# First-block transposes of x and g moved to TensorE, second-block transposing loads spread over ticks, and dwq computed for two heads at once, in an attention forward and backward kernel

## Chip, cores and metric

One core of a Trainium2 chip. The metric is the device time of one execution in microseconds (us). A ratio is the mean time of one kernel's fast runs over the mean of the other's fast runs of the same rounds, so it is not quite the ratio of the medians that stand beside it. Times are compared only within a set.

## The reference

Two independent attention blocks A and B with a key and value cache; output and all gradients are wanted. B=8 batches, 96 query rows, D=640, H=32 heads, 512 cached keys, head size 128, bfloat16. For one block:

```python
q = (x @ wq).reshape(B, Sq, H, Dh).transpose(0, 2, 1, 3)
p = softmax(einsum("bhqd,bhkd->bhqk", q, k_cache) * Dh ** -0.5)
o = einsum("bhqk,bhkd->bhqd", p, v_cache)
out = o.transpose(0, 2, 1, 3).reshape(B, Sq, H * Dh) @ wo
# gradients: d x, d k_cache, d v_cache, d wq, d wo; the outputs of A and B are concatenated
```

## The kernel before

The program is a software pipeline. A *tick* is one (head, batch) pair: 256 ticks for block A, 256 for B. Every piece of work is put at a tick and a slot, sorted, and issued in that order on each engine. Heads come in pairs (16 ticks) and in groups of four (32 ticks), so the pattern of work repeats every 32 ticks. `HK` says in which tick, counted from the start of a pair, the work of a head stands: pA loads its weights, pB transposes them, pC projects q and dO, pD makes natural tiles, qA transposes O (0) and dQ (1) back, qB computes dwo, qD computes dwq.

```python
HK = [
    dict(pA=-10, pB=-7, pC0=[-6, -4], pC1=[-5, -3], pD1=-2, pD0=0, qA0=21, qA1=25, qB=[28, 25], qD=[(26, 0, 2), (27, 2, 5)]),
    dict(pA=-7, pB=-2, pC0=[-1, 3], pC1=[1, 2], pD1=3, pD0=6, qA0=29, qA1=33, qB=[36, 33], qD=[(34, 0, 2), (35, 2, 5)]),
]
# ... cut ...
    def setup_T(which_, c):          # xT or gT: 128 columns of x or grad_out, transposed on the way in
        def f():
            # ... cut: the tile, one buffer ...
            sp(nc.sync.dma_start_transpose(S[key][:, c, :], src_flat[:, c * 128:(c + 1) * 128]))
        return f
# ... cut ...
    for c in range(DC):              # DC = 5
        em.add(tick0 + (-10 if first else -11 + c // 3), SL_LOAD + 0.5, setup_T(0, c))
        em.add(tick0 + (-9 if first else -10 + (c + 1) // 3), SL_LOAD + 0.6, setup_T(1, c))
    em.add(tick0 + (8 if first else 22), SL_LOAD + 0.5, setup_nat(1))   # g_nat, 960 KB
    em.add(tick0 + (9 if first else 21), SL_LOAD + 0.5, setup_nat(0))   # x_nat, 960 KB
# ... cut ...
            for ci in range(ncn):    # qD: dwq of one head, 128 columns wide
                c = c_lo + ci
                for t in range(TT):  # TT = 6
                    nc.tensor.matmul(w_ps[:, ci * 128:(ci + 1) * 128], S["x_nat"][:, t, c * 128:(c + 1) * 128], dQnat[:, t * 128:(t + 1) * 128],
                                     start=(t == 0), stop=(t == TT - 1))
# ... cut ...
            j = h % HP               # c_s7: dK of two heads is evicted into one tile and stored
            if j == 0:
                st["dK_p"] = wk.tile([128, HP, KC * 128], BF16, name="dK_sb", bufs=3)
```

All loads and stores are issued from one in-order queue (`sp`).

Names used below: S_ps holds the scores q k^T of one tick, negm their negated row maximum, E_sb the exponentials, P_sb the probabilities, PT_sb their transpose, dS_sb the gradient of the scores. KT_p and VT_p are keys and values transposed on the way in, K_sb and V_sb the same as they lie in memory. x_nat and g_nat are x and grad_out as they lie in memory ("natural" tiles), xT and gT their transposes. dV_sb and dK_sb are gradients that wait to be stored. To evict is to copy a result of TensorE from its accumulator to working memory.

Of the kernel before, what the change touches and what calls it, by code (L numbers as in the profile page):

```python
# [10 lines left out]
F32 = mybir.dt.float32  # L11
BF16 = mybir.dt.bfloat16
# [3 lines left out]
class Emitter:  # L16
# [14 lines left out]
SL_LOAD = 0  # L31
# [8 lines left out]
SL_HEAD = 90  # L40
SL_GRP = 95
SL_SETUP = 96

OFF = dict(kt=-1, vt=2, vn=1, kn=4, dv=7, dk=10, s2=3, s3=3, s4=4, s5=5, s6=6, s7=7, s8=8)
HP = 2
HK = [
    dict(pA=-10, pB=-7, pC0=[-6, -4], pC1=[-5, -3], pD1=-2, pD0=0, qA0=21, qA1=25, qB=[28, 25], qD=[(26, 0, 2), (27, 2, 5)]),
    dict(pA=-7, pB=-2, pC0=[-1, 3], pC1=[1, 2], pD1=3, pD0=6, qA0=29, qA1=33, qB=[36, 33], qD=[(34, 0, 2), (35, 2, 5)]),
]
EV = dict(pB0="act", pB1="dve", pC00="act", pC01="act", pC10="act", pC11="dve", pD0="dve", pD1="dve", qA0="dve", qA1="dve", qB0="act", qB1="act", qD="dve", gU="act")  # L50
GSPREAD0 = 9
# [20 lines left out]
def build_block(tc, em, tick0, blk, x, kc, vc, wq, wo, g_all, out_all, dx, dk, dv, dwq, dwo, ident, ones, pools, HG=4, first=True, groups=None):  # L72
    nc = tc.nc
    B, Sq, D = x.shape
# [4 lines left out]
    TT = T // 128  # L79
# [32 lines left out]
    def bank(shape, dt, name):  # L112
        return ps.tile(shape, dt, name=name, tag="bank")
# [8 lines left out]
    def setup_T(which_, c):  # L122
        def f():
            key = "xT" if which_ == 0 else "gT"
            if c == 0:
                S[key] = const.tile([128, DC, T], BF16, name=key, bufs=1)
            src_flat = x_flat if which_ == 0 else g_flat
            sp(nc.sync.dma_start_transpose(S[key][:, c, :], src_flat[:, c * 128:(c + 1) * 128]))
        return f

    def setup_nat(which_):
        def f():
            key = "x_nat" if which_ == 0 else "g_nat"
            src_flat = x_flat if which_ == 0 else g_flat
            t_ = const.tile([128, TT, D], BF16, name=key, bufs=1)
            sp(nc.sync.dma_start(t_[:], src_flat.rearrange("(t p) d -> p t d", p=128)))
            S[key] = t_
        return f
# [3 lines left out]
            S["out_acc"] = const.tile([128, TT, D], F32, name="out_acc", bufs=1)  # L142
            S["dx_acc"] = const.tile([128, TT, D], F32, name="dx_acc", bufs=1)

    for c in range(DC):
        em.add(tick0 + (-10 if first else -11 + c // 3), SL_LOAD + 0.5, setup_T(0, c))
        em.add(tick0 + (-9 if first else -10 + (c + 1) // 3), SL_LOAD + 0.6, setup_T(1, c))
    em.add(tick0 + (8 if first else 22), SL_LOAD + 0.5, setup_nat(1))
    em.add(tick0 + (9 if first else 21), SL_LOAD + 0.5, setup_nat(0))

    def evac(eng, dst, src, sc=None):
        if eng == "act":
            nc.scalar.activation(dst, src, ACT.Identity, scale=(1.0 if sc is None else sc))
        else:
            if sc is None:
                nc.vector.tensor_copy(dst, src)
            else:
                nc.vector.tensor_scalar(dst, src, float(sc), None, op0=ALU.mult)

    def pA(h):  # L160
        def f():
            g, hh = h // HG, h % HG
            if hh == 0:
                G[g] = dict(wo_r=grp.tile([128, HG, D], BF16, name="wo_r", bufs=2))
            wo_h = G[g]["wo_r"][:, hh]
            sp(nc.sync.dma_start(wo_h, wo[h * 128:(h + 1) * 128, :]))
            j = h % HP
            if j == 0:
                wq_p = hd.tile([128, DC, HP * 128], BF16, name="wq_p", bufs=2)
                with nc.allow_non_contiguous_dma(reason="per-pair wq slice"):  # L170
                    sp(nc.sync.dma_start(wq_p[:], wq_v[:, :, h * 128:(h + HP) * 128]))
            else:
                wq_p = HS[(blk, h - j)]["wq_p"]
            HS[(blk, h)] = dict(wo_h=wo_h, wq_p=wq_p, wq_h=wq_p[:, :, j * 128:(j + 1) * 128])
        return f
# [248 lines left out]
    def qA(h, which):  # L424
        def f():
            st = HS[(blk, h)]
            src = st["OT_h"] if which == 0 else st["dQT_h"]
            dst = hd.tile([128, TT * 128], BF16, name="Onat" if which == 0 else "dQnat", bufs=1)
            st["Onat" if which == 0 else "dQnat"] = dst
            for t0 in range(0, TT, 8):  # L430
                nt = min(8, TT - t0)
                n_ps = bank([128, 8 * 128], BF16, "nat_ps")
                for i in range(nt):
                    nc.tensor.transpose(n_ps[:, i * 128:(i + 1) * 128], src[:, (t0 + i) * 128:(t0 + i + 1) * 128], ident[:])  # L434
                evac(EV["qA%d" % which], dst[:, t0 * 128:(t0 + nt) * 128], n_ps[:, 0:nt * 128])
        return f

    def qB(h, di):
        def f():
            st = HS[(blk, h)]  # L440
            Onat = st["Onat"]
            if "dwo_sb" not in st:
                st["dwo_sb"] = hd.tile([128, D], BF16, name="dwo_sb")
            dwo_sb = st["dwo_sb"]
            (c0, w) = dsplits[di]
            w_ps = bank([128, w], F32, "dwo_ps")
            for t in range(TT):
                nc.tensor.matmul(w_ps[:], Onat[:, t * 128:(t + 1) * 128], S["g_nat"][:, t, c0:c0 + w], start=(t == 0), stop=(t == TT - 1))  # L448
            evac(EV["qB%d" % di], dwo_sb[:, c0:c0 + w], w_ps[:])
        return f  # L450

    def qB_st(h):
        def f():
            sp(nc.sync.dma_start(dwo[h * 128:(h + 1) * 128, :], HS[(blk, h)]["dwo_sb"][:]))
        return f

    def qD(h, c_lo, c_hi):
        def f():
            st = HS[(blk, h)]
            dQnat = st["dQnat"]  # L460
            j = h % HP
            pr = HS[(blk, h - j)]
            if "dwq_sb" not in pr:
                pr["dwq_sb"] = hd.tile([128, DC, HP * 128], BF16, name="dwq_sb", bufs=1)
            dwq_sb = pr["dwq_sb"]
            ncn = c_hi - c_lo
            w_ps = bank([128, 4 * 128], F32, "dwq_ps")
            for ci in range(ncn):
                c = c_lo + ci
                for t in range(TT):  # L470
                    nc.tensor.matmul(w_ps[:, ci * 128:(ci + 1) * 128], S["x_nat"][:, t, c * 128:(c + 1) * 128], dQnat[:, t * 128:(t + 1) * 128],  # L471
                                     start=(t == 0), stop=(t == TT - 1))
            evac(EV["qD"], dwq_sb[:, c_lo:c_hi, j * 128:(j + 1) * 128], w_ps[:, 0:ncn * 128].rearrange("p (a b) -> p a b", b=128))
        return f

    def qD_st(h):
        def f():
            with nc.allow_non_contiguous_dma(reason="per-pair dwq slice"):
                sp(nc.sync.dma_start(dwq_v[:, :, h * 128:(h + HP) * 128], HS[(blk, h)]["dwq_sb"][:]))
        return f  # L480
# [7 lines left out]
    def gU(g, which, t, di):  # L488
        def f():
            acc = S.get("out_acc" if which == 0 else "dx_acc")  # L490
            (c0, w) = dsplits[di]
            o_ps = bank([128, w], F32, "o_ps")
            for hh in range(groups[g]):
                h = GH0[g] + hh
                src = HS[(blk, h)]["OT_h"] if which == 0 else HS[(blk, h)]["dQT_h"]
                rhs = G[g]["wo_r"][:, hh, c0:c0 + w] if which == 0 else HS[(blk, h)]["wqT_h"][:, c0:c0 + w]
                nc.tensor.matmul(o_ps[:], src[:, t * 128:(t + 1) * 128], rhs, start=(hh == 0), stop=(hh == groups[g] - 1))  # L497
            if g == NG - 1:
                if di == 0:
                    G[(g, which, t)] = wk.tile([128, D], BF16, name="ob", bufs=4)  # L500
                dst = G[(g, which, t)][:, c0:c0 + w]
            else:
                dst = acc[:, t, c0:c0 + w]
            if g == 0:
                evac(EV["gU"], dst, o_ps[:])
            else:
                nc.vector.tensor_tensor(dst, o_ps[:], acc[:, t, c0:c0 + w], op=ALU.add)  # L507
        return f
# [10 lines left out]
    for g in range(NG):  # L519
        h0 = GH0[g]  # L520
        for hh in range(groups[g]):
# [1 line left out]
            j = h % HP  # L523
            c0t = tick0 + (h - j) * B
            hk = HK[j]
            em.add(c0t + hk["pA"], SL_LOAD, pA(h))
            em.add(c0t + hk["pB"], SL_HEAD, pB(h))
            em.add(c0t + OFF["s5"], SL_LOAD, h_alloc(h))
            for si in range(NTS):
# [27 lines left out]
            for di in range(len(dsplits)):  # L557
                em.add(c0t + hk["qB"][min(di, len(hk["qB"]) - 1)], SL_HEAD + 1, qB(h, di))
            em.add(c0t + max(hk["qB"]) + 2, SL_LOAD + 0.3, qB_st(h))
            if j == HP - 1:  # L560
                em.add(c0t + max(q[0] for q in hk["qD"]) + 2, SL_LOAD + 0.3, qD_st(h - j))
            em.add(c0t + hk["qA1"], SL_HEAD, qA(h, 1))
            for (k_, c_lo, c_hi) in hk["qD"]:
                if c_lo < DC:
                    em.add(c0t + k_, SL_HEAD + 2, qD(h, c_lo, min(c_hi, DC)))
        cLg = tick0 + (h0 + groups[g]) * B - 1
        gs0 = max(3, (GSPREAD0 * groups[g]) // HG)
        gs1 = max(3, (GSPREAD1 * groups[g]) // HG)
# [131 lines left out]
```

## Time and profile before

| | before |
|---|---|
| median at first, three runs | 1703.83 us (1701.45 to 1710.41) |
| span of the profiled run | 1698.9 us |
| first S_ps matmul | 24.04 us |
| 32 ticks in steady state | 102.14 us, 3.19 us a tick |
| hole at the boundary of the blocks | TensorE stands still about 5 us, then runs slow |

The page of the kernel before, parts 1, 2 and 3. Part 1 gives busy time, share of the span and instruction count; the digits of part 2 are tenths.

```profile
span 1698.9 us, 57158 instructions
PE 1622.0 (95%) x21526; PEld 1277.7 (75%) x21760; DVE 1363.6 (80%) x3409; ACT 1344.4 (79%) x3505; POOL 535.1 (31%) x1030
...
DMA  9999999999999999999999999999999999999994
...
q1 hardware_dynamic: 386112, 456.54, 102.0%
```

TensorE (PE) is at 95% and the DMA engines look full nearly everywhere.

The timeline of the kernel before, at its start (start us, duration us, engine or queue, line, operation), and two S_ps matmuls 32 ticks apart in steady state.

```profile
1.66 6.51 SPq L128 DMA_TRANSPOSE xT<-in_A_x_dram  x5
...
8.21 6.57 SPq L128 DMA_TRANSPOSE gT<-in_grad_out_dram  x5
...
15.45 2.39 SPq L239 DMA_TRANSPOSE KT_p<-in_A_k_cache_dram  x2
...
24.04 0.38 PE L279 MATMUL S_ps<-KT_p,QT_h 128*96 128x512 bf16 x1
...
324.30 0.38 PE L279 MATMUL S_ps<-KT_p,QT_h 128*96 128x512 bf16 x1
...
395.07 0.34 PE L400 MATMUL dq_dst_ps<-ident,dS_sb 96*128 96x96 bf16 x4 [0.20 <-DVE dS_sb L378]
...
397.41 0.34 PE L400 MATMUL dq_dst_ps<-ident,dS_sb 96*128 96x96 bf16 x4 [0.51 <-DVE dS_sb L378]
...
426.44 0.38 PE L279 MATMUL S_ps<-KT_p,QT_h 128*96 128x512 bf16 x1
```

Ten transposing loads hold the queue for 13 us before the first key load can be issued.

The windows view of the kernel before: length, busy us (and instructions) of each engine, granted clock, DMA share, GB/s. First two steady stretches of 102 us, then the boundary.

```profile
428.90:531.00 102.10, 100.11 (x1347) 79.37 (x1360) 85.85 (x217) 82.75 (x217) 33.37 (x64) 1.00 1.01 267
531.00:633.20 102.20, 100.21 (x1348) 79.45 (x1362) 85.97 (x218) 82.84 (x217) 33.40 (x65) 1.00 1.05 276
...
810.00:815.00 5.00, 4.31 (x55) 3.04 (x52) 2.60 (x8) 2.98 (x8) 1.05 (x2) 1.00 1.02 194
815.00:820.00 5.00, 1.41 (x6) 0.51 (x5) 0.98 (x3) 0.38 (x2) 1.02 (x2) 1.00 1.14 234
820.00:825.00 5.00, 3.83 (x38) 3.55 (x38) 1.67 (x4) 3.15 (x8) 0.67 (x1) 0.51 0.82 264
825.00:830.00 5.00, 4.95 (x50) 3.62 (x49) 2.35 (x6) 3.40 (x9) 0.94 (x3) 0.81 1.09 270
```

In steady state TensorE is 98% busy. At the boundary it stops, and the granted clock falls to 0.51 and 0.81 afterwards. The Trainium skill, "TensorE: Matmul & The Clock Gate" (Part 1: The HAM clock gate), says that an idle window of about 3.4 us puts the array back to half its clock. The stop at the boundary, 3.76 us in the timeline, fits that. But in the same trace the clock also halved at a shorter stop (0.50 in the windows view from 137.4 to 140.8 us):

```profile
137.94 0.69 PE L182 MATMUL woT_ps<-ident,wo_r 128*128 128x128 bf16 x5 [2.79 <-ACT dK_sb L421]
```

So the trace agrees only in part; how short a stop is enough was not measured. At the boundary, ScalarE's timeline names what stopped TensorE:

```profile
813.63 0.60 ACT L355 ACTIVATE dV_sb<-dV_ps 128x512 bf16<-128x512 f32 x1 [2.02 <-DMA out_dram<-dV_sb]
...
820.53 0.60 ACT L421 ACTIVATE dK_sb<-dK_ps 128x512 bf16<-128x512 f32 x1 [5.15 <-DMA out_dram<-dK_sb]
```

The stores were issued behind ten transposing loads (792 to 814 us in the queue's timeline), so their buffers came free late.

### The profile page before, as it was taken

How to read it: one execution, taken by the hardware profiler on the slowest of the kernel's cores; microseconds unless marked ns; L12 is line 12 of the kernel's file. 1: busy time of each engine (PE TensorE's matmuls, PEld its weight loads, DVE VectorE, ACT ScalarE, POOL GpSimd, SP SyncE). 2: the span in 40 equal slices, each digit the busy share in tenths (PEclk: the TensorE clock that was granted, in tenths of full speed). 3: DMA queues.
4: the chain of work that ended last, by engine and by line, in shares of the span. 5: the costliest groups of instructions: out<-in, count | busy, mean ns of one | idle time of the engine just before them, and what ended most of it. 6: DMA issues, size and time to landing. Idle time of an engine off the chain costs nothing. (4 is left out here: it accounts for less than half of the span.)

```text
span 1698.9 us, 57158 instructions
## 1 busy us (share of the span) xinstructions
PE 1622.0 (95%) x21526; PEld 1277.7 (75%) x21760; DVE 1363.6 (80%) x3409; ACT 1344.4 (79%) x3505; POOL 535.1 (31%) x1030
## 2 busy tenths in 40 slices
PE   6899999999999999999899899999999999999998
PEld 4676777877778777777777677777787777777776
DVE  3776788888888888888687768888888888878886
ACT  4888887878778787887777889778787878878783
POOL 1332333333333233333233323333332333323331
PEclk9999999999999999999999999999999999999999
DMA  9999999999999999999999999999999999999994
GB/s 224 283 253 291 274 270 270 271 291 274 282 262 273 277 281 255 270 292 255 259 292 304 290 267 274 279 284 260 273 274 283 263 277 257 276 288 265 293 267 160
DMA packets 386390, 460.21 MB, mean 271 GB/s; under 512 B 52288, under 2 KB 377920, under 8 KB 377920
## 3 DMA queue, kind: packets, MB, share of 16 engines
q1 hardware_dynamic: 386112, 456.54, 102.0%
q8 instruction: 170, 2.79, 0.7%
q14 instruction: 108, 0.88, 0.1%
HBM read 159.12 MB, written 159.12 MB: 187 GB/s over the span
## 5 line engine op out<-in xcount | busy, mean ns | idle before, releaser
L310 POOL TENSOR_SCALAR P_sb<-E_sb,rinv 96x512 bf16<-96x512 bf16 x512 | 353.7, 691 | 491.7 <-DVE rinv L301 490.4
L291 ACT ACTIVATE E_sb<-S_ps,negm 96x512 bf16<-96x512 f32 x512 | 349.2, 682 | 132.9 <-DVE negm L281 130.4
L421 ACT ACTIVATE dK_sb<-dK_ps 128x512 bf16<-128x512 f32 x512 | 303.7, 593 | 156.8 <-PE dK_ps L416 128.2
L378 DVE SCALAR_TENSOR_TENSOR dS_sb<-dP_ps,dl_ps,P_sb 96x512 bf16<-96x512 f32 x512 | 383.3, 749 | 40.0 <-PE dl_ps L376 23.3
L281 DVE TENSOR_REDUCE negm<-S_ps 96x1 f32<-96x512 f32 x512 | 347.2, 678 | 66.0 <-PE S_ps L279 65.1
L364 POOL TENSOR_TENSOR prod<-OT_h,dOT_h 128x96 bf16<-128x96 bf16 x512 | 187.1, 366 | 643.9 <-DVE OT_h L336 639.7
L355 ACT ACTIVATE dV_sb<-dV_ps 128x512 bf16<-128x512 f32 x512 | 308.1, 602 | 3.9 <-DMA out_dram<-dV_sb 3.0
L339 ACT ACTIVATE PT_sb<-optp_ps 128x384 bf16<-128x384 bf16 x512 | 252.1, 492 | 0.5 <-PE optp_ps L333 0.5
L279 PE MATMUL S_ps<-KT_p,QT_h 128*96 128x512 bf16 x512 | 194.4, 380 | 10.7 <-ACT dK_sb L421 8.9
L350 PE MATMUL dV_ps<-dOnat_h,P_sb 96*128 96x128 bf16 x2048 | 198.4, 219 | 0.0
L416 PE MATMUL dK_ps<-Qnat_h,dS_sb 96*128 96x128 bf16 x2048 | 198.3, 219 | 0.0
L374 PE MATMUL dP_ps<-VT_p,dOT_h 128*96 128x512 bf16 x512 | 195.4, 382 | 0.6 <-ACT dV_sb L355 0.6
L400 PE MATMUL dq_dst_ps<-ident,dS_sb 96*128 96x96 bf16 x2048 | 173.2, 207 | 21.7 <-DVE dS_sb L378 19.5
L402 DVE COPY dST_sb<-dq_dst_ps 128x384 bf16<-128x384 bf16 x512 | 177.1, 346 | 14.0 <-PE dq_dst_ps L400 13.9
L333 PE MATMUL optp_ps<-ident,P_sb 96*128 96x96 bf16 x2048 | 172.0, 205 | 4.2 <-POOL P_sb L310 1.6
L326 PE MATMUL optp_ps<-PT_sb,V_sb 128*128 128x96 bf16 x2048 | 172.1, 206 | 0.9 <-ACT PT_sb L339 0.8
L393 PE MATMUL dq_dst_ps<-dST_sb,K_sb 128*128 128x96 bf16 x2048 | 171.1, 206 | 0.0
L393 PEld LDWEIGHTS <-K_sb 128*128 128x128 bf16 x2048 | 131.5, 98 | 38.6 <-issue 1.0
L497 PE MATMUL o_ps<-wqT_h,dQT_h 128*128 128x128 bf16 (+1 forms) x706 | 143.2, 292 | 3.3
L497 PE MATMUL o_ps<-wo_r,OT_h 128*128 128x128 bf16 (+1 forms) x707 | 142.5, 294 | 3.5 <-issue 0.4
L336 DVE CAST OT_h<-optp_ps 128x96 bf16<-128x96 f32 x512 | 126.1, 246 | 21.5 <-PE optp_ps L333 17.8
L400 PEld LDWEIGHTS <-dS_sb 96*128 96x128 bf16 x2048 | 114.3, 98 | 33.7 <-DVE dS_sb L378 32.3
(58 smaller groups left out, 3064.2 us busy)
## 6 DMA issues: line engine op xcount, KB each, us to landing
out_dram<-dV_sb SPq DMA_DIRECT2D x256, 256.0 KB, 4.6
out_dram<-dK_sb SPq DMA_DIRECT2D x256, 256.0 KB, 4.6
V_sb<-in_A_v_cache_dram SPq DMA_DIRECT2D x128, 256.0 KB, 4.5
K_sb<-in_A_k_cache_dram SPq DMA_DIRECT2D x128, 256.0 KB, 4.6
V_sb<-in_B_v_cache_dram SPq DMA_DIRECT2D x128, 256.0 KB, 4.3
K_sb<-in_B_k_cache_dram SPq DMA_DIRECT2D x128, 256.0 KB, 4.7
out_dram<-dwo_sb SPq DMA_DIRECT2D x64, 160.0 KB, 4.6
out_dram<-dwq_sb SPq DMA_DIRECT2D x32, 320.0 KB, 4.1
```

The source lines that it names most:

```text
L281: nc.vector.tensor_reduce(negm[:], S_ps[:], axis=AX.X, op=ALU.max, negate=True)
L291: nc.scalar.activation(E_sb[:].rearrange("q (a f) -> q a f", f=F4), st["S_ps"][:].rearrange("q (f a) -> q a f", f=F4), ACT.Exp, bias=st["n ...
L310: nc.gpsimd.tensor_scalar(P_sb[:], st["E_sb"][:], st["rinv"][:], 0.0, op0=ALU.mult, op1=ALU.add)
L339: nc.scalar.activation(PT_sb[:], PT_ps, ACT.Identity, scale=1.0)
L350: nc.tensor.matmul(dV_ps[:, c * 128:(c + 1) * 128], P_sb[:, c * 128:(c + 1) * 128], hs["dOnat_h"][:, b * 128:(b + 1) * 128], start=True, s ...
L355: nc.scalar.activation(dV_p[:, j], dV_ps[:], ACT.Identity, scale=1.0)
L378: nc.vector.scalar_tensor_tensor(dS_sb[:].rearrange("q (a f) -> q a f", f=F4), dP_ps[:].rearrange("q (f a) -> q a f", f=F4), dl_ps[:, 0:1] ...
L393: nc.tensor.matmul(dQT_ps, st["K_sb"][:, c, :], st["dST_sb"][:, c * Sq:(c + 1) * Sq], start=(c == 0), stop=(c == KC - 1))
L400: nc.tensor.transpose(dST_ps[:, c * Sq:(c + 1) * Sq], dS_sb[:, c * 128:(c + 1) * 128], ident[0:Sq, 0:Sq])
L416: nc.tensor.matmul(dK_ps[:, c * 128:(c + 1) * 128], dS_sb[:, c * 128:(c + 1) * 128], hs["Qnat_h"][:, b * 128:(b + 1) * 128], start=True, s ...
L421: nc.scalar.activation(dK_p[:, j], dK_ps[:], ACT.Identity, scale=1.0)
L497: nc.tensor.matmul(o_ps[:], src[:, t * 128:(t + 1) * 128], rhs, start=(hh == 0), stop=(hh == groups[g] - 1))
```

## The change

Three intents: no transposing loads at the start, because the natural tiles that are needed anyway can be loaded first and transposed on TensorE; the same loads of the second block spread over more ticks, so that they do not block the queue; and dwq of a pair of heads with matmuls twice as wide. Some buffer counts fall (ob 4 to 3, dwo_sb 2 to 1). The core of the diff:

```diff
-    ... qD=[(26, 0, 2), (27, 2, 5)]),
-    dict(... pC0=[-1, 3], pC1=[1, 2], ... qD=[(34, 0, 2), (35, 2, 5)]),
+    ...),
+    dict(... pC0=[-1, 1], pC1=[0, 2], ... qD=[(37, 0, 2), (38, 2, 4), (39, 4, 5)]),
@@ setup_T
-            sp(nc.sync.dma_start_transpose(...))
+            if not first:
+                sp(nc.sync.dma_start_transpose(...))
+                return
+            pt = bank([128, TT * 128], BF16, "tp_ps")
+            for t in range(TT):
+                nc.tensor.transpose(pt[:, t * 128:(t + 1) * 128], S["x_nat" if which_ == 0 else "g_nat"][:, t, c * 128:(c + 1) * 128], ident[:])
+            evac("act" if c % 2 == 0 else "dve", S[key][:, c, :], pt[:])
@@ schedule of these loads
+    if first:
+        em.add(tick0 - 14, SL_LOAD, setup_nat(0))
+        em.add(tick0 - 14, SL_LOAD, setup_nat(1))
+        for c in range(DC):
+            em.add(tick0 - 9, SL_SETUP, setup_T(0, c))
+            em.add(tick0 - 8, SL_SETUP, setup_T(1, c))
+    else:
+        for i in range(2 * DC):
+            em.add(tick0 - 13 + (2 * i) // 3, SL_LOAD + 0.5, setup_T(i // DC, i % DC))
+        em.add(tick0 + 22, SL_LOAD + 0.5, setup_nat(1))
+        em.add(tick0 + 25, SL_LOAD + 0.5, setup_nat(0))
@@ qD, now once for a pair
-                    nc.tensor.matmul(w_ps[:, ci * 128:(ci + 1) * 128], ..., dQnat[:, t * 128:(t + 1) * 128], ...)
+                    nc.tensor.matmul(w_ps[:, ci, :], ..., dQnat[:, t, :], ...)   # 256 columns
```

The first lines also move dwq, and two pieces of the projections, to other ticks.

More of the change, by code (lines that the diff above doesn't have):

```diff
@@ L46 @@
 HK = [
-    dict(pA=-10, pB=-7, pC0=[-6, -4], pC1=[-5, -3], pD1=-2, pD0=0, qA0=21, qA1=25, qB=[28, 25], qD=[(26, 0, 2), (27, 2, 5)]),
-    dict(pA=-7, pB=-2, pC0=[-1, 3], pC1=[1, 2], pD1=3, pD0=6, qA0=29, qA1=33, qB=[36, 33], qD=[(34, 0, 2), (35, 2, 5)]),
+    dict(pA=-10, pB=-7, pC0=[-6, -4], pC1=[-5, -3], pD1=-2, pD0=0, qA0=21, qA1=25, qB=[28, 25]),
+    dict(pA=-7, pB=-2, pC0=[-1, 1], pC1=[0, 2], pD1=3, pD0=6, qA0=29, qA1=33, qB=[36, 33], qD=[(37, 0, 2), (38, 2, 4), (39, 4, 5)]),
 ]
@@ L127, in f @@
             src_flat = x_flat if which_ == 0 else g_flat
-            sp(nc.sync.dma_start_transpose(S[key][:, c, :], src_flat[:, c * 128:(c + 1) * 128]))
+            if not first:
+                sp(nc.sync.dma_start_transpose(S[key][:, c, :], src_flat[:, c * 128:(c + 1) * 128]))
+                return
[3 more added lines that the diff above has]
+            evac("act" if c % 2 == 0 else "dve", S[key][:, c, :], pt[:])
         return f
@@ L143, in setup_acc @@
             S["dx_acc"] = const.tile([128, TT, D], F32, name="dx_acc", bufs=1)
-    for c in range(DC):
-        em.add(tick0 + (-10 if first else -11 + c // 3), SL_LOAD + 0.5, setup_T(0, c))
-        em.add(tick0 + (-9 if first else -10 + (c + 1) // 3), SL_LOAD + 0.6, setup_T(1, c))
-    em.add(tick0 + (8 if first else 22), SL_LOAD + 0.5, setup_nat(1))
-    em.add(tick0 + (9 if first else 21), SL_LOAD + 0.5, setup_nat(0))
     def evac(eng, dst, src, sc=None):
@@ L427, in f @@
             src = st["OT_h"] if which == 0 else st["dQT_h"]
-            dst = hd.tile([128, TT * 128], BF16, name="Onat" if which == 0 else "dQnat", bufs=1)
-            st["Onat" if which == 0 else "dQnat"] = dst
-            for t0 in range(0, TT, 8):
-                nt = min(8, TT - t0)
-                n_ps = bank([128, 8 * 128], BF16, "nat_ps")
-                for i in range(nt):
-                    nc.tensor.transpose(n_ps[:, i * 128:(i + 1) * 128], src[:, (t0 + i) * 128:(t0 + i + 1) * 128], ident[:])
-                evac(EV["qA%d" % which], dst[:, t0 * 128:(t0 + nt) * 128], n_ps[:, 0:nt * 128])
+            j = h % HP
+            if which == 0:
+                dst = hd.tile([128, TT, 128], BF16, name="Onat", bufs=1)
+                st["Onat"] = dst
+                view = dst[:]
+            else:
+                pr = HS[(blk, h - j)]
+                if j == 0:
+                    pr["dQnat"] = hd.tile([128, TT, HP * 128], BF16, name="dQnat", bufs=1)
+                view = pr["dQnat"][:, :, j * 128:(j + 1) * 128]
+            n_ps = bank([128, TT * 128], BF16, "nat_ps")
+            for i in range(TT):
+                nc.tensor.transpose(n_ps[:, i * 128:(i + 1) * 128], src[:, i * 128:(i + 1) * 128], ident[:])
+            evac(EV["qA%d" % which], view, n_ps[:].rearrange("p (t d) -> p t d", d=128))
         return f
@@ L442, in f @@
             if "dwo_sb" not in st:
-                st["dwo_sb"] = hd.tile([128, D], BF16, name="dwo_sb")
+                st["dwo_sb"] = hd.tile([128, D], BF16, name="dwo_sb", bufs=1)
             dwo_sb = st["dwo_sb"]
@@ L447, in f @@
             for t in range(TT):
-                nc.tensor.matmul(w_ps[:], Onat[:, t * 128:(t + 1) * 128], S["g_nat"][:, t, c0:c0 + w], start=(t == 0), stop=(t == TT - 1))
+                nc.tensor.matmul(w_ps[:], Onat[:, t, :], S["g_nat"][:, t, c0:c0 + w], start=(t == 0), stop=(t == TT - 1))
             evac(EV["qB%d" % di], dwo_sb[:, c0:c0 + w], w_ps[:])
@@ L458, in f @@
         def f():
-            st = HS[(blk, h)]
-            dQnat = st["dQnat"]
-            j = h % HP
-            pr = HS[(blk, h - j)]
+            pr = HS[(blk, h)]
+            dQnat = pr["dQnat"]
             if "dwq_sb" not in pr:
                 pr["dwq_sb"] = hd.tile([128, DC, HP * 128], BF16, name="dwq_sb", bufs=1)
-            dwq_sb = pr["dwq_sb"]
-            ncn = c_hi - c_lo
-            w_ps = bank([128, 4 * 128], F32, "dwq_ps")
-            for ci in range(ncn):
+            n = c_hi - c_lo
+            w_ps = bank([128, 2, HP * 128], F32, "dwq_ps")
+            for ci in range(n):
                 c = c_lo + ci
                 for t in range(TT):
-                    nc.tensor.matmul(w_ps[:, ci * 128:(ci + 1) * 128], S["x_nat"][:, t, c * 128:(c + 1) * 128], dQnat[:, t * 128:(t + 1) * 128],
-                                     start=(t == 0), stop=(t == TT - 1))
-            evac(EV["qD"], dwq_sb[:, c_lo:c_hi, j * 128:(j + 1) * 128], w_ps[:, 0:ncn * 128].rearrange("p (a b) -> p a b", b=128))
+                    nc.tensor.matmul(w_ps[:, ci, :], S["x_nat"][:, t, c * 128:(c + 1) * 128], dQnat[:, t, :], start=(t == 0), stop=(t == TT - 1))
+            evac(EV["qD"], pr["dwq_sb"][:, c_lo:c_hi, :], w_ps[:, 0:n, :])
         return f
@@ L499, in f @@
                 if di == 0:
-                    G[(g, which, t)] = wk.tile([128, D], BF16, name="ob", bufs=4)
+                    G[(g, which, t)] = wk.tile([128, D], BF16, name="ob", bufs=3)
                 dst = G[(g, which, t)][:, c0:c0 + w]
@@ L525, in build_block @@
             hk = HK[j]
-            em.add(c0t + hk["pA"], SL_LOAD, pA(h))
+            em.add(c0t + (hk["pA"] if h > 0 or not first else -15), SL_LOAD, pA(h))
             em.add(c0t + hk["pB"], SL_HEAD, pB(h))
@@ L559, in build_block @@
             em.add(c0t + max(hk["qB"]) + 2, SL_LOAD + 0.3, qB_st(h))
+            em.add(c0t + hk["qA1"], SL_HEAD, qA(h, 1))
             if j == HP - 1:
-                em.add(c0t + max(q[0] for q in hk["qD"]) + 2, SL_LOAD + 0.3, qD_st(h - j))
-            em.add(c0t + hk["qA1"], SL_HEAD, qA(h, 1))
-            for (k_, c_lo, c_hi) in hk["qD"]:
-                if c_lo < DC:
-                    em.add(c0t + k_, SL_HEAD + 2, qD(h, c_lo, min(c_hi, DC)))
+                for (k_, c_lo, c_hi) in hk["qD"]:
+                    em.add(c0t + k_, SL_HEAD + 2, qD(h - j, c_lo, min(c_hi, DC)))
+                em.add(c0t + k_ + 2, SL_LOAD + 0.3, qD_st(h - j))
         cLg = tick0 + (h0 + groups[g]) * B - 1
```

## The prediction

> **What bounds it now.** The windows view splits the 1698.9 us span into three regimes.
> - Steady state (300-700 us): TensorE is 98% busy at full clock, 31.5 ticks (head, batch) per 100 us, 3.17 us each. In the waits view nothing stops TensorE for long: it is the bound.
> - First group (20-140 us): no grouped projection work yet, so TensorE needs less per tick, but ticks still take about 3.2 us (37 dS_sb operations in 120 us). TensorE is 68-99% busy by slice, the DMA share is 1.0-1.1 at 260-287 GB/s. DMA is the bound; between 20 and 150 us TensorE idles 18 us. In this stretch x_nat and g_nat (1.97 MB, issued at 38 and 34 us) compete with the k/v loads.
> - Two holes. Start: ten transposing loads occupy the DMA queue from 1.66 to 14.78 us (about 1.3 us each), k loads start only at 15.45, the first S_ps at 24.04. Five xT loads move 0.98 MB in 6.5 us, 151 GB/s; the Trainium skill, "DMA: Bandwidth & Descriptors" (Latency and other measured facts), gives 261 GB/s for a DMA transpose with a non-contiguous middle dimension; this trace is slower. Boundary: ten such loads in three ticks hold the queue 793-814 us, the dV and dK stores are issued late behind them, ScalarE waits 2.0 and 5.15 us for those stores, TensorE stops 0.6 + 0.9 + 3.8 us and then runs at clock 0.51 and 0.81 in the next two 5 us slices: about 9 us lost.
>
> **Change, part by part.**
> 1. First block: the ten transposing loads go, the two natural loads (needed anyway) move to about 2 us. Added: 60 TensorE transposes (5 of them took 0.71 us cold, 0.44 warm: 5-8 us) and ten evictions 128x768 (0.54 us on VectorE; about 0.8 on ScalarE, estimated from 0.71 for 128x640). At 270-300 GB/s (estimate) g_nat lands near 10-11 us, so preparing two heads still follows; first S_ps at about 21.5 us, 2.5 us earlier. The queue is free for k/v at about 3 us instead of 15, and 1.97 MB less is moved in the DMA-bound stretch: 1.97 MB / 276 GB/s = 7 us. Gain 9 us (4 to 14), all critical.
> 2. Second block: two or one transposing loads a tick. Ordinary issues cost about 2.1 us of queue per tick (1.17 per transpose, 0.41-0.58 per plain), plus 1.4 x 1.35 makes 4.0 against 3.2 for seven ticks: 6 us short instead of 10, mostly covered by the buffers' lead. The hole shrinks from 9 to about 3 us and the clock holds. Gain 6 us (2 to 9).
> 3. dwq: 960 matmuls of 256 columns for 1920 of 128. Columns are the same; 12 dwq matmuls ran in 0.67-0.69 us, 56 ns each. The Trainium skill, "TensorE: Matmul & The Clock Gate" (Back-to-back issue gap) puts N/2.4 + 2.5 ns on each, which agrees: 960 x 2.5 ns = 2.4 us. Halved weight loads are hidden already. VectorE saves some 5 us off the path. Filling emptier ticks may remove about 1 us of waits for dS_sb. Gain 3 us (0 to 5).
> Fewer buffers (ob, dwo_sb): no cost expected; the tail moves under 1 us.
>
> Sum: 1703.8 - 18 = 1686 us, 8 in 10 between 1674 and 1698. Chances: faster by over 2% 0.10, within 2% 0.88, slower 0.02.
>
> **Signs.** First S_ps at 21-22 us; TensorE idle in 20-150 us down from 18 to near 10; no store wait over 3 us and clock 1.00 at the boundary; the tick in 300-700 us still 3.15-3.17 us.
>
> **What would make it wrong.** The first group is limited by store order, not DMA bytes, so the 7 us does not come; TensorE transposes wait serially on evictions; spreading only lengthens the queue shortage; dwq bunched in three ticks makes new waits for dS_sb.

## More of the kernel before

A cycle is 32 ticks; a quiet cycle is one that no late transfer lengthens.

The 32-tick cycle is 426.44 - 324.30 = 102.14 us. It has two ticks in a row in which TensorE waits for VectorE's dS_sb.

## The result

| | before | after |
|---|---|---|
| median | 1703.49 us (4 runs) | 1677.13 us (1674.12 to 1680.38, 4 runs) |
| ratio | | 0.9839, 95% interval 0.9805 to 0.9872 |
| span of the profiled run | 1698.9 us | 1672.3 us |
| first S_ps | 24.04 us | 21.79 us |
| 32 ticks in steady state | 102.14 us | 100.81 us |

The time lies inside the predicted range and the class "within 2%" holds, but the gain is about 26 us where 18 were forecast. The page of the kernel after, parts 1, 2 and 3:

```profile
span 1672.3 us, 55383 instructions
PE 1607.8 (96%) x20640; PEld 1265.2 (76%) x20860; DVE 1366.7 (82%) x3381; ACT 1336.2 (80%) x3511; POOL 533.8 (32%) x1030
...
DMA  9999999999999999999999999999999999999994
...
q1 hardware_dynamic: 378112, 454.57, 102.3%
```

The timeline of the kernel after, at the same places:

```profile
1.66 0.52 SPq L142 DMA_DIRECT2D x_nat<-in_A_x_dram  x1
...
2.22 0.55 SPq L142 DMA_DIRECT2D g_nat<-in_grad_out_dram  x1
...
4.26 6.73 SPq L251 DMA_TRANSPOSE KT_p<-in_A_k_cache_dram  x2
...
21.79 0.38 PE L291 MATMUL S_ps<-KT_p,QT_h 128*96 128x512 bf16 x1
...
309.47 0.38 PE L291 MATMUL S_ps<-KT_p,QT_h 128*96 128x512 bf16 x1
...
383.33 0.34 PE L412 MATMUL dq_dst_ps<-ident,dS_sb 96*128 96x96 bf16 x4 [0.52 <-DVE dS_sb L390]
...
410.28 0.38 PE L291 MATMUL S_ps<-KT_p,QT_h 128*96 128x512 bf16 x1
...
797.08 0.38 PE L224 MATMUL q_ps<-gT,woT_h 128*128 128x512 bf16 x1 [2.53 <-DMA gT<-in_grad_out_dram]
...
802.96 0.59 PE L224 MATMUL q_ps<-gT,woT_h 128*128 128x512 bf16 x1 [5.51 <-DMA gT<-in_grad_out_dram]
```

The key loads are in the queue at 4.26 instead of 15.45 us. The 32-tick cycle is 410.28 - 309.47 = 100.81 us, with one visible wait for dS_sb where there were two. And at the boundary TensorE now waits 2.5 + 5.5 us for the last two gT loads. The windows view of the kernel after, a steady stretch and the boundary:

```profile
513.70:614.50 100.80, 99.28 (x1287) 78.31 (x1300) 85.82 (x215) 81.94 (x217) 33.24 (x65) 1.00 1.06 276
...
795.00:800.00 5.00, 0.38 (x1) 0.10 (x1) 0.09 (x1) 1.47 (x3) 0.00 (x0) 0.73 0.96 289
800.00:805.00 5.00, 2.04 (x21) 1.76 (x21) 0.36 (x1) 1.41 (x5) 0.00 (x0) 0.50 1.03 263
805.00:810.00 5.00, 4.95 (x46) 3.52 (x45) 2.26 (x7) 3.13 (x8) 1.28 (x3) 0.74 1.40 361
```

The hole is as large as before. Where the time went is best read from a ledger: the start of the n-th P_sb operation (one per tick) in each trace, and by how much the kernel after is ahead.

| tick | before, us | after, us | ahead, us | with the new start alone (e1) | with new dwq and ticks alone (e2) |
|---|---|---|---|---|---|
| 0 | 26.6 | 24.0 | 2.6 | 3.2 | 0.2 |
| 48 | 176.7 | 164.0 | 12.7 | 9.5 | 6.5 |
| 64 | 224.6 | 211.3 | 13.3 | 9.5 | 6.8 |
| 224 | 735.3 | 715.5 | 19.9 | 9.2 | 12.8 |
| 320 | 1059.3 | 1037.5 | 21.8 | 9.0 | 16.7 |
| 511 | 1666.8 | 1637.5 | 29.3 | 9.9 | 24.2 |
| end of the span | 1698.9 | 1672.3 | 26.6 | 9.8 | 21.6 |

A gain at the start, a steady gain of 6.6 us in 160 ticks of block A and 7.5 us in the last 191 ticks, 2 us from tick 224 to 320, across the boundary (where steady ticks alone would give 4), and 2.7 us lost in the tail. Each column is one execution. Five profiles whose programs are the same up to there (after, e4, e5, e11, e12, on several chips) reach tick 48 at 163.8 to 167.0 us, so a difference of 3 us between two columns means little.

There is a second hole, which the prediction does not have. In the kernel after, the cycle that follows the one with the boundary (ticks 256 to 288) takes 109.89 us where a quiet one takes 100.81; in the kernel before two cycles share the loss, 105.90 and 106.96 against 102.14. TensorE stops there, in the kernel after:

```profile
917.90 0.59 PE L291 MATMUL S_ps<-KT_p,QT_h 128*96 128x512 bf16 x1 [5.23 <-ACT dK_sb L433]
```

ScalarE had itself waited 4.91 us for a store of dK, after the natural loads of block B were issued (892 and 907 us). No run took these loads away, so their part in it is not shown.

### The profile page after: what moved, and what is told of

It is laid out like the page before. It is cut to its first block, busy times and chain, and to the rows that moved or that the text cites. A ratio compares the mean times of both kernels' runs of the same rounds, so it can differ in the third digit from the quotient of the medians.

```text
span 1672.3 us, 55383 instructions
## 1 busy us (share of the span) xinstructions
PE 1607.8 (96%) x20640; PEld 1265.2 (76%) x20860; DVE 1366.7 (82%) x3381; ACT 1336.2 (80%) x3511; POOL 533.8 (32%) x1030
## 4 chain that ended last, share of the span: by engine, by line
PE 88%; DVE 5%; DMA 2%; issue 2%; ACT 2%; POOL 0%; SPq 0%; ACTq 0%; DVEq 0%
PE q_ps L224 12%; PE o_ps L511 11%; PE dK_ps L428 6%; PE dV_ps L362 6%; PE dP_ps L386 6%; PE S_ps L291 6%; PE dwo_ps L466 6%; PE dwq_ps L486 6%; PE dq_dst_ps L412 5%; PE optp_ps L345 5%; PE optp_ps L338 5%; PE dq_dst_ps L405 4%; PE n_ps L239 4%; PE nat_ps L452 3%; DVE dS_sb L390 2%
## 5 line engine op out<-in xcount | busy, mean ns | idle before, releaser
L390 DVE SCALAR_TENSOR_TENSOR dS_sb<-dP_ps,dl_ps,P_sb 96x512 bf16<-96x512 f32 x512 | 383.2, 748 | 29.0 <-PE dl_ps L388 18.6
L224 PE MATMUL q_ps<-gT,woT_h 128*128 128x256 bf16 (+1 forms) x609 | 134.4, 324 | 9.7 <-DMA gT<-in_grad_out_dram 8.0
```

The costliest lines, as they stand in the source:

```text
L224: nc.tensor.matmul(q_ps[:], lhs(c), rhsT[:, c, t0:t0 + w], start=(c == 0), stop=(c == DC - 1))
L390: nc.vector.scalar_tensor_tensor(dS_sb[:].rearrange("q (a f) -> q a f", f=F4), dP_ps[:].rearrange("q (f a) -> q a f", f=F4), dl_ps[:, 0:1] ...
```

## The experiments

Theory: the start gives 9 to 13 us, the spread of the loads nothing, and most of the rest comes from *where* dwq stands in the ticks and not from its width. Rival: the prediction's sizes (9, 6 and 3 us), or width as the real cause. The first four runs shared one set of runs of the kernel before (median 1705.73 us).

**e1_start.** The kernel before with the new start only (natural loads first, TensorE transposes, pA of head 0 earlier).

> The kernel before with only the first block's new start (natural loads first, transposes of x and g on TensorE). Theory: the start alone carries 11 to 13 us of the gain (the traces of before and after stand 11.9 us apart at tick 32), so ratio about 0.993; the tick in steady state stays at 3.19 to 3.20 us. Rival (the prediction): 9 us, ratio 0.9947. If the gain at tick 32 in the full change came from the tick schedule and not from the start, this run gains only the 2.6 us of the earlier first tick.

Measured: 1691.23 us, ratio 0.9919 (0.9896 to 0.9942). The ledger's e1 column: 3.2 us at tick 0, 9.5 at tick 48, then flat to the end. The start is worth 9 to 10 us by this one trace; the prediction's 9 fits. The theory's 11 to 13 was too much: at tick 32 this run was 6.5 us ahead, the full change 11.9, so in the first group part of the full gain probably came from the tick schedule (e2 alone was 1.2 us ahead there). The ratio alone would give 14 us, with an interval of plus or minus 4.

**e2_dwq.** The kernel before with the new dwq and tick places, old start, old boundary loads (x_nat of block B at tick 25, as after, because dwq needs the old one longer).

```diff
-    for the loads: the schedule of the kernel after
+    for the loads: the schedule of the kernel before, x_nat of block B at tick0 + 25
```

> The kernel before with only dwq for two heads at once and the tick places that go with it (pC0, pC1, qD), old start and old boundary loads. Theory: the steady tick falls from 3.199 to about 3.151 us and the run gains 15 to 20 us less the 2 to 3 us that the tail lost, ratio 0.988 to 0.992. Rival (the prediction): 2.4 us of fixed cost per matmul plus at most 2 us of waits, ratio 0.9975 or higher.

Measured: 1681.13 us, ratio 0.9865 (0.9839 to 0.9892), a little better than the theory's range; undisturbed 32-tick cycles of 100.81 us. The prediction's value for this part (3 us) is refuted. The tail is 34.7 us from tick 511 to the end against 32.1 in the kernel before, so the lost 2.6 us belong to this part.

**e3_ticks.** e2 with narrow matmuls in the same ticks.

```diff
-                for t in range(TT):
-                    nc.tensor.matmul(w_ps[:, ci, :], ..., dQnat[:, t, :], ...)
+                for j in range(HP):
+                    for t in range(TT):
+                        nc.tensor.matmul(w_ps[:, ci, j * 128:(j + 1) * 128], ..., dQnat[:, t, j * 128:(j + 1) * 128], ...)
```

> As e2, the same places in the ticks, but every dwq matmul stays 128 columns wide (1920 of them). Theory: the gain of e2 comes from where the work stands in the ticks, not from wide matmuls; the tick is 3.156 us, 4.9 ns above e2 (2.5 ns for each of 1.9 saved matmuls a tick), and the run is within 4 us of e2. Rival (wide matmuls or fewer weight loads matter): the tick goes back to 3.19 us and nearly all the gain of e2 is gone.

Measured: 1693.79 us (1688.49 to 1704.13), ratio 0.9930 (0.9900 to 0.9959): 12.7 us slower than e2, outside what the theory allowed. But its trace, taken of its slowest execution, shows two kinds of 32-tick cycle: 100.94 us in quiet ones, as the theory said, and 101.4 to 105.6 us in others. In the disturbed ones ScalarE waits for a store of dK. Its timeline, three of these waits:

```profile
343.59 0.60 ACT L421 ACTIVATE dK_sb<-dK_ps 128x512 bf16<-128x512 f32 x1 [2.57 <-DMA out_dram<-dK_sb]
...
515.08 0.60 ACT L421 ACTIVATE dK_sb<-dK_ps 128x512 bf16<-128x512 f32 x1 [2.17 <-DMA out_dram<-dK_sb]
...
1273.37 0.60 ACT L421 ACTIVATE dK_sb<-dK_ps 128x512 bf16<-128x512 f32 x1 [3.28 <-DMA out_dram<-dK_sb]
```

There were 25 such waits with 43.0 us in sum, against 10 with 16.7 us in e2. So the run told two effects apart only in its trace; e8 and e9 were made for the rest.

**e4_bunch.** The kernel after with block B's transposing loads in three ticks again.

```diff
-            em.add(tick0 - 13 + (2 * i) // 3, SL_LOAD + 0.5, setup_T(i // DC, i % DC))
+            em.add(tick0 - 11 + c // 3, SL_LOAD + 0.5, setup_T(0, c))
+            em.add(tick0 - 10 + (c + 1) // 3, SL_LOAD + 0.6, setup_T(1, c))
```

> The kernel after with the second block's transposing loads bunched in three ticks again. Theory: the spread moved the hole from waiting on the dK store to waiting on the last gT load and gained nothing, so this run is within 2 us of after (ratio to before 0.984), with a hole of 7 to 10 us at the boundary. Rival (the prediction): the spread is worth 6 us, so this run is 6 us slower than after (ratio to before 0.9875).

Measured: 1676.38 us, ratio 0.9829 (0.9801 to 0.9858), against 0.9839 for the kernel after. The cycle that holds the boundary takes 111.37 us here and 111.34 us in the kernel after (111.10 before). The waits view of e4 between 775 and 830 us shows the old reason back:

```profile
ACT dK_sb L434 <- DMA out_dram<-dK_sb: 6.8, 2, 5.0
```

The spread changed which wait ends last, the dK store or the gT load, and did not shorten the cycle. Over all profiles the boundary cycle takes 108.0 to 113.8 us with bunched loads (before, e1 to e4, e8) and 111.3 to 116.2 us with spread ones (after, e6, e7, e9, e10, e12), chips mixed. The predicted 6 us are refuted.

The next four ran on another chip, where the kernel before had a median of 1714.94 us.

**e5_stage.** The kernel after with block B's transposing loads replaced by plain loads of 128 rows and TensorE transposes (six buffers shared with ob, which is idle then).

```diff
-            em.add(tick0 - 13 + (2 * i) // 3, SL_LOAD + 0.5, setup_T(i // DC, i % DC))
+        for t in range(TT):
+            em.add(tick0 - 15 + t, SL_LOAD + 0.5, stage_ld(0, t))   # 160 KB each, x
+            em.add(tick0 - 14 + t, SL_LOAD + 0.5, stage_ld(1, t))   # and g
+            em.add(tick0 - 13 + t, SL_HEAD + 3, stage_T(0, t))      # 5 transposes, 1 eviction
+            em.add(tick0 - 12 + t, SL_HEAD + 3, stage_T(1, t))
```

> The kernel after with the second block's ten transposing loads replaced by twelve plain loads of 160 KB (0.5 us of queue each instead of 1.35) and 60 TensorE transposes, one x and one g piece per tick. Theory: the boundary hole (5.5 us wait for the last gT load, 6 to 8 us with the cold clock after it) comes from the time that the transposing loads take in the one DMA queue, so it vanishes; the 60 transposes cost 3.4 us. Net gain of 3 to 6 us on after, ratio to before about 0.981, TensorE busy above 95% in every 5 us slice around the boundary. Rival: the boundary is short of DMA bandwidth, which these loads use as well; then a hole of 5 us or more stays and the run is level with or slower than after.

Measured: 1679.46 us, ratio 0.9789 (0.9754 to 0.9824). The boundary cycle takes 104.93 us. Repeated as e11 below.

**e6_reload.** The kernel after, reading x and g of block A a second time into scratch.

> The kernel after with x and g of the first block read a second time (1.97 MB in twelve plain loads, nobody waits for them) in ticks 6 to 11, about where the kernel before read them. Theory (the prediction's 7 us): the first group is bound by the bytes moved, so this costs about 7 us (1.97 MB at 276 GB/s) by tick 40, and the run is 6 to 8 us slower than after (ratio to before 0.988). Rival: the DMA queues have room there and the gain of the start was only the earlier first tick and the free queue; then the run is within 2 us of after.

Measured: 1698.32 us, ratio 0.9908 (0.9878 to 0.9937). The total would suit the theory, but the trace does not: against e5, which is the same program up to the boundary and ran on the same chip, this run is 4.5 us behind at tick 24 and only 0.8 us behind at tick 40. The rest of the difference in total comes from disturbed cycles and the boundary. So 1.97 MB more in the first group do not cost 7 us by its end: it reaches tick 40 at 139.3 us, and the five profiles without the extra loads reach it at 136.2 to 139.4. The prediction's term of bytes over rate is not confirmed, and the rival is not either, since 4.5 us were lost for a while. There was no control on this chip, so the total decides nothing.

**e7_buf.** The kernel after with four buffers for dK_sb and dV_sb.

```diff
-                st["dK_p"] = wk.tile([128, HP, KC * 128], BF16, name="dK_sb", bufs=3)
+                st["dK_p"] = wk.tile([128, HP, KC * 128], BF16, name="dK_sb", bufs=4)   # dV_sb likewise
```

> The kernel after with four instead of three buffers for dK_sb and dV_sb. Theory: stores that land late stop ScalarE only because there are three buffers (three such waits, 10.4 us, in the profile of after, 4.9 us of it near 915 us); with four they vanish and the run gains 3 to 5 us (ratio to before 0.981). Rival: the waits only move to the next buffer that is full; then no change beyond 1 us.

Measured: 1696.55 us, ratio 0.9885 (0.9857 to 0.9912): no gain; by ratio slower than the kernel after, though on another chip. The waits for dK stores are nearly gone (2.5 us in 2 waits; e5 and e6, on the same chip with three buffers, had 33.8 and 36.8 us), and others stand in their place, as the rival said. The waits view (us in total, times, longest):

```profile
PEld L291 <- DMA KT_p<-in_A_k_cache_dram: 11.7, 7, 3.9
PEld L405 <- DMA K_sb<-in_B_k_cache_dram: 9.7, 6, 6.1
ACT dwo_sb L153 <- DMA out_dram<-dwo_sb: 8.9, 7, 2.9
```

In the kernel after no wait for K_sb was in the list. With three buffers the wait is for a store, with four it is for a load. It did help in one place: at tick 40 this run stood at 132.7 us against 138.5 and 139.3 in e5 and e6 on the same chip, so in the first group late stores seem to be part of what limits (one profile; e8 and e3, which differ in these buffers but ran on different chips, are 0.4 us apart there).

**e8_ticks_buf.** e3 with four buffers.

> e3 (tick places of the change, narrow dwq matmuls) with four buffers for dK_sb and dV_sb. Theory: e3 lost its gain to 25 waits of ScalarE for dK stores, 43 us in sum, which depend on chance meetings in the DMA queues and not on the width; with four buffers they vanish, the tick is 3.155 us and the run comes within 4 us of e2 (1681 us, ratio 0.9865). Rival: width itself matters; then it stays near e3 (1694 us, ratio 0.993).

Measured: 1708.91 us, ratio 0.9977 (0.9945 to 1.0009). The expectation failed: four buffers do not bring e3 to e2's level, and the waits move to KT and K_sb loads as in e7. It is a failure of the cure, not a proof for width; quiet cycles are 100.94 us here too.

The last four ran on a third chip, kernel before 1710.25 us, with the kernel after as control.

**e12_after.** Control.

> The kernel after, unchanged, as the control on this chip. Ratio to before 0.984 as in its first timing; undisturbed 32-tick cycles of 100.81 us against 102.14 in before. If the chip's DMA is as slow as that of the second set, some cycles are lengthened by late dK stores to 102 to 104 us and the ratio is 0.985 to 0.99.

Measured: 1682.77 us, ratio 0.9847 (0.9819 to 0.9875). The first result repeats. Quiet cycles 100.81 us; disturbed ones, 101.9 to 104.0 us, in block A.

**e9_narrow.** The kernel after with narrow dwq matmuls, same ticks (the diff of e3).

> After with 1920 narrow dwq matmuls in the same ticks. Theory: width is worth 2.5 ns for each of the 960 extra matmuls, an undisturbed cycle of 100.94 to 100.96 us, and the run is 2 to 4 us slower than the control. Rival (e3 was 12.7 us slower than e2 on the same chip): narrow matmuls somehow bring the late stores, and the run is 8 us or more slower than the control.

Measured: 1685.10 us, ratio 0.9860 (0.9827 to 0.9894), 2.3 us slower than the control by median; quiet cycles 100.95 us. That is 0.14 us in 32 ticks, or 4.6 ns a tick; 2.5 ns for each of 60 matmuls saved in 32 ticks gives 0.15 us. The intervals of the totals overlap; the cycle decides. Width is worth what the prediction said. For the kernel after, the rival that e3 had raised falls.

**e10_place.** The kernel after with the wide dwq matmuls three ticks earlier.

```diff
-    ... qD=[(37, 0, 2), (38, 2, 4), (39, 4, 5)]),
+    ... qD=[(34, 0, 2), (35, 2, 4), (36, 4, 5)]),
```

> After with the wide dwq matmuls three ticks earlier (ticks 34 to 36 in place of 37 to 39 of a pair), the same work and the same loads. Theory: the gain of the steady state comes from filling the ticks 5 to 8 of each 16, in which TensorE would otherwise have less work than the chain over VectorE and ScalarE takes; emptied again, TensorE waits for dS_sb and P_sb there, the 32-tick cycle goes from 100.8 to 101.8 or more and the run is 10 to 16 us slower than the control. Rival (width, fewer evictions or fewer weight loads give the gain): the cycle stays within 0.2 us of 100.8.

Measured: 1692.93 us, ratio 0.9897 (0.9867 to 0.9927), 10.2 us slower than the control by median (the intervals just overlap); quiet cycles 101.83 us. The second wait for dS_sb is back; in e10's timeline, at the place shown for the other two kernels:

```profile
386.48 0.34 PE L412 MATMUL dq_dst_ps<-ident,dS_sb 96*128 96x96 bf16 x4 [0.20 <-DVE dS_sb L390]
...
388.82 0.34 PE L412 MATMUL dq_dst_ps<-ident,dS_sb 96*128 96x96 bf16 x4 [0.51 <-DVE dS_sb L390]
```

The visible waits are only part of it. A table of start-to-start times of TensorE's instructions over one quiet cycle (tick 416 to 448), in ns per tick, shows the rest. Each row holds four matmuls and the wait of the next instruction behind them:

| group, and what the next one needs | before | after | e10 |
|---|---|---|---|
| dQ matmuls, then transposes of dS_sb | 225.3 | 208.6 | 222.9 |
| O matmuls, then transposes of P_sb | 184.0 | 172.5 | 184.0 |
| dK matmuls, then O matmuls on PT_sb | 227.2 | 223.4 | 227.2 |
| whole tick | 3192.0 | 3150.2 | 3182.1 |

These three rows make 29.6 of the 31.9 ns by which e10's tick is longer than that of the kernel after. The busy time in the windows view hides about half of it. One quiet cycle of e10, then one of the control:

```profile
1354.53:1456.36 101.83, 100.61 (x1302) 78.52 (x1301) 85.72 (x215) 82.48 (x218) 33.42 (x65) 1.00 1.01 270
...
1343.37:1444.18 100.81, 100.04 (x1301) 78.38 (x1300) 86.03 (x215) 82.06 (x218) 33.45 (x65) 1.00 1.06 286
```

TensorE is busy for 100.61 us here and for 100.04 us in the control, for the same matmuls: a matmul's modelled end runs past the next one's start (a matmul of 512 columns is recorded as 0.38 us, and the next one starts 0.22 us after it did), and short waits vanish inside it. (The first profile of the kernel after shows only 99.28 us, but there 14 of the 1300 matmul records of each quiet cycle are missing; it is not to be compared with these.) The Trainium skill, "Trainium Kernel Development and Optimization" (Performance Expectations), says that matmul busy time is a bad measure and that the weight-load share is a good one. This agrees: weight loads are busy 78.52 us of 101.83 in e10 and 78.38 of 100.81 in the control.

**e11_stage.** The kernel of e5 again, beside the control.

> The kernel of e5 again, now beside the control. Theory: the boundary hole is gone, which is worth 4 to 8 us: ratio to before 0.979 to 0.981, and below the control's by 0.003 to 0.005. Rival: e5 stood out from e7 only because e7's buffers hurt it; then it is within 2 us of the control.

Measured: 1680.53 us (1665.66 to 1684.20), ratio 0.9819 (0.9782 to 0.9856), 2.2 us below the control; the intervals overlap. The boundary itself is repaired, as the windows view of e11 shows:

```profile
795.00:800.00 5.00, 5.00 (x66) 4.17 (x65) 4.59 (x13) 3.60 (x11) 1.31 (x3) 1.00 1.26 310
800.00:805.00 5.00, 4.73 (x78) 4.20 (x77) 4.47 (x11) 4.46 (x12) 1.83 (x4) 1.00 0.79 244
805.00:810.00 5.00, 5.00 (x70) 3.88 (x67) 4.79 (x14) 4.84 (x15) 2.05 (x4) 1.00 1.05 235
```

No stop, and the clock stays at 1.00. The cycle with the boundary takes 104.24 us, against 114.13 in the control's profile and 111.34 in the first profile of the kernel after. The rival for the boundary (a shortage of bandwidth) falls: the same bytes, loaded plainly, fit. One thing was not told apart: these loads also stand two ticks earlier (-15 to -9 instead of -13 to -7), so part of it may be their lead. The total gains little for two reasons. The next cycle, that of the second hole, takes 110.61 us here and 103.35 in the control, so of 9.9 us at the boundary 2.6 are left after the two cycles. And block A had four disturbed cycles of 103.0 to 105.1 us in this profile, against 101.9 to 104.0 in the control, that have nothing to do with the boundary. Whether e11 beats the kernel after is not shown.

## Why the prediction was right or wrong

**1. The start: right in size, its second reason not confirmed.** Predicted 9 us, measured 9.5 us at tick 48 of e1. First S_ps at 21.79 us (21 to 22 predicted), TensorE idle between 20 and 150 us down from 18.6 to 11.6 us (18 to near 10 predicted). The first tick comes 2.6 to 3.2 us earlier, as said. The other term, "1.97 MB / 276 GB/s = 7 us", did not show in e6. What else brings the remaining 6 us is not settled; e7 hints that late stores are part of the limit in the first group, which the prediction had named as its risk.

**2. The boundary: wrong.** The failed step is "6 us short instead of 10, mostly covered by the buffers' lead". Spread or bunched, the boundary cycle takes 111.3 to 111.4 us (after, e4). Each transposing load still holds the queue for 1.2 to 1.9 us, and the last gT load stands at tick -7 for a use at tick -5. The queue fell behind TensorE until those loads themselves were late: 2.5 and 5.5 us of waiting, and the clock then at 0.73, 0.50 and 0.74. "Spreading only lengthens the queue shortage" had been listed as a way to be wrong, and is what happened. Taking the transposing loads away (e11, with two ticks more lead) closed the hole; spreading them did not.

**3. dwq: the width was right, the placement was mis-sized.** "960 x 2.5 ns = 2.4 us" agrees with e9 (0.14 us in each of 16 cycles, 2.2 us). The failed term is "filling emptier ticks may remove about 1 us". It removes about 1 us *in every 32 ticks*. A 32-tick cycle went from 102.14 to 100.81 us: 1.33 us. Of this, 1.02 come from the ticks where dwq stands (e10 against after; e10 uses ticks 34 to 36, not the exact old places), 0.14 from its width (e9 against after), and the remaining 0.17, if the parts add, from what both leave untouched, among it the moved projections, which no run moved alone. Over 16 such cycles it would be 21 us. The waits that went are those for dS_sb, P_sb and PT_sb (the table of e10): in the emptied ticks TensorE had less to do than the chain S_ps, negm, E_sb, P_sb and dS_sb takes on VectorE, ScalarE and GpSimd, and waited for it. The waits view hardly shows this in the rows of the matmuls, but it does in those of the weight loads. First the kernel before, then the kernel after:

```profile
PE dq_dst_ps L400 <- DVE dS_sb L378: 19.5, 53, 1.6
PEld L400 <- DVE dS_sb L378: 32.3, 73, 1.7
...
PE dq_dst_ps L412 <- DVE dS_sb L390: 20.3, 43, 1.3
PEld L412 <- DVE dS_sb L390: 27.0, 45, 1.5
```

e10 has 34.6 us in the weight-load row. The matmul row does not see waits that are hidden under the modelled end of a matmul. One sign of the prediction misleads here: "the tick in 300-700 us still 3.15-3.17 us" came out at 3.150 us, but as a fall, since the tick before was 3.192 us and not 3.17.

**4. The tail.** Predicted under 1 us, measured 2.7 us lost. Every profile with dwq at its new ticks has a tail of 34.7 to 35.0 us, before and e1 have 32.1 and 32.2; with dwq three ticks earlier (e10) it is 33.8, so about 1 us belongs to the later dwq. The rest (fewer ob buffers, or other) was not tested.

**5. The sum.** 9 + 6 + 3 was 18; the traces give 9.8 us from the start and 21.6 from dwq and ticks if each is done alone, 0 from the boundary, and together 26.6. That the total fell inside the range was partly luck: 6 us too much at the boundary stood against 14 to 19 us too few for dwq and its ticks (26.6 less e1's 9.8, or e2's 21.6, where 3 were said). The parts do not add, 31.4 against 26.6. By the ledger 3.3 of these 4.8 us are missing at tick 48 already: both parts help the same first group. This is no more than the spread between profiles there, so it is not shown. Late stores lengthen some cycles by 1 to 4 us in e12, e5 and e11, and hardly any in the first profile of the kernel after, in e2 and e4, or at the longer cycle of before and e1. The former three ran on other chips, where the kernel before was not profiled, so whether the shorter cycle, the chip or chance brings them is not shown. In steady state "it is the bound" was true of TensorE; the waits of e12, e5 and e11 suggest that the DMA comes next.

Open: why e3 was slower than e2 in all of its executions (1688.49 us at the least against 1687.16 at the most); whether bytes or order limit the first group; what makes the second hole.

## What to carry to other kernels

When TensorE bounds a pipeline that repeats, look at the length of one period and at the start-to-start times within it, not at busy shares or listed waits: moving the same work into the ticks where the softmax chain is the slower one gave seven times what the wider matmuls gave. Spreading expensive DMA issues does not help if the sum of the queue's time over the stretch stays too long; replace them by cheaper ones, and look at the next cycle too, where part of the gain can be lost again. When the first bound shrinks, look for the second one, here probably the DMA; in e7 and e8 a fourth buffer only chose which wait showed it.

## What the Trainium skill lacked or had wrong

- "DMA: Bandwidth & Descriptors" (Latency and other measured facts) gives 261 GB/s for a DMA transpose with a non-contiguous middle dimension and 350 to 400 GB/s for the contiguous case. Five loads of 128 columns by 768 rows (gT, at 8.21 us in the kernel before) moved 0.98 MB in 6.57 us here, 150 GB/s, with nothing else issued meanwhile; the queue was issuing all that time, so it may be the issue and not the transfer that sets this rate.
- The same page (Issuing engines are not separate DMA queues) calls the issuing time usually small against the DMA itself. Each such transposing load held the issuing queue for about 1.3 us (plain ones mostly 0.4 to 0.6 us), and ten of them were enough to stop TensorE for 5 to 8 us at the block boundary.
- "TensorE: Matmul & The Clock Gate" (Back-to-back issue gap): its formula for one matmul, N/2.4 + 2.5 ns, was confirmed: about 2.5 ns per matmul saved by wider moving operands, 0.14 us for 60 matmuls. The larger figure that it gives for a stream with weight loads, about 81 ns at 128 columns, was not: the narrow dwq matmuls of the kernel before start 56 ns apart. Its idle window (Part 1) was longer than the 2.79 us stop at which the clock halved here.
- No page says that matmul busy time can *rise* with waiting for the same work: 100.61 us in e10 against 100.04 us in e12.
